# Exponentials on VectorE as a sum of two terms, masks over pairs of steps, 109 steps instead of 99

## The chip, the cores and the metric

The kernel runs on one core of a Trainium2 chip. The core has engines that run side by side: TensorE (PE, with its weight loads as PEld), VectorE (DVE), ScalarE (ACT), GpSimd (POOL) and SyncE (SP, which here only starts transfers). Each works through its own queue in order and waits on semaphores of the others. The metric is the time of one execution on the device in microseconds (us); lower is better. A profile is one traced execution.

## The reference, cut to what matters

Two attention layers read the same x (2048 rows, 512 columns, 32 heads of 16) and are mixed by a gate. A is linear attention with softmax features, B is full softmax attention.

```python
qkv = (x @ wqkv).reshape(B, S, 3, H, Dh)            # in both layers, each with its weights
# A: phi(q), phi(k) = softmax features of q @ w_phi, k @ w_phi (both signs, 32 per head)
num = phi_q @ (phi_k^T @ v);  den = phi_q . sum(phi_k) + 1e-6;  a = (num / den) @ wo_A
# B:
scores = einsum("bhqd,bhkd->bhqk", q, k) * (Dh ** -0.5)
b = einsum("bhqk,bhkd->bhqd", softmax(scores), v) @ wo_B
out = g * a + (1 - g) * b                           # g = sigmoid((x * gate_w).sum(-1))
```

B needs 32 x 2048 x 2048 exponentials. They are most of the work.

## The kernel before

**Tiling of B.** The work is cut into 32 sets: four chunks of 512 queries (`qc`), four groups of eight heads (`g`), and the even or odd heads of a group (`par`). A set has four heads and 16 steps, one for each 128 keys (`kt`). A step has two halves. In each half, TensorE writes the scores of two heads into a score buffer of PSUM (`R_r`, 128 x 1024 floats, three buffers; L736; `qk`). Then one of two engines takes the exponentials:

- ScalarE reads a score buffer and writes 128 x 1024 exponentials in bf16 to an `E` buffer (L755; ring `E_r`, six buffers; in the first set also memory that is not in use yet, `phiK` and `vA`).
- VectorE, for `NDVE` of the 16 steps of a set, builds the exponentials out of the bits of a bf16 number. L745 adds a constant to the scores, which were scaled so that the integer result, read as bf16, has the right exponent (`I`, two halves of a step in one buffer of 2048 columns). L760 keeps the exponent bits (`G`), L763 the mantissa bits (`F`), L766 squares `F`, L769 multiplies `I` by `F`. The exponential is the sum of three terms, I, G and F, of which the last two are weighted by `CPOLY`.

The sum itself is made by TensorE: the value products (`pv`; L791 for ScalarE's steps, L778 for VectorE's) multiply the exponentials by V with columns of ones beside it and accumulate all steps of a set in one PSUM bank (`O_r`, one buffer). VectorE's steps take three products of four matmuls each: I with `vB`, G and F with `vC`, a copy of V times `CPOLY` for the first four key steps (L518). At the end of a set VectorE copies the bank out (`OT`, L453), and it is transposed (L816) and divided by its sum (L820, L827).

**Beside it** run the projections (L459), the features of A (exponentials on ScalarE L621, their sums on VectorE L623 and L627, their division on GpSimd L628), checks of the denominators on GpSimd (L625, L822 to L826) and the output (L867 to L885). A query tile has one copy of q per head of four with the other rows zero: GpSimd clears three of the four query buffers (L430), transfers scatter q into them (L503, `qsp`); the first query tile is instead built by VectorE by four products with masks (L494).

**What sets the order.** The queues are written out by a scheduler in Python (`_Sched`): every operation has an engine, an assumed duration, a due time (`prio`), a time before which it is not placed (`nb`) and the buffers it takes. The scheduler plays these through with its own clock and puts each operation on its engine's queue. Only the resulting order and the waits for semaphores reach the chip, not the planned times. `next_pe` picks TensorE's next operation by a rank: scores for ScalarE when fewer than two or three lie ahead of it, then scores for VectorE, then the rest by due time. `T0`, `tset` and `ut` give the calendar of the sets; `LEAD` is how much earlier than its place in the set a VectorE step begins.

```python
NDVE = [0, 1] + [3, 3, 3, 4] * 7 + [3, 4]
R_r = _Slots([ps[:, 1024 * i:1024 * (i + 1)] for i in range(3)])
O_r = _Slots([ps[:, 3072:3584]])
```

At the end a check of the denominators (`flag`) decides whether a slow second version runs; it did not in the profile.

Of the kernel before, what the change touches and what calls it, by code (L numbers as in the profile page):

```python
# [6 lines left out]
BF16 = mybir.dt.bfloat16  # L7
# [6 lines left out]
D = 512  # L14
H = 32
# [11 lines left out]
CPOLY = 0.65625  # L27
KAP = 2.1484825
# [4 lines left out]
ND = 4  # L33
# [3 lines left out]
NDVE = [0, 1] + [3, 3, 3, 4] * 7 + [3, 4]  # L37
LEAD = 5.0
EXTRA = 1.2
SLACK = 0.8  # L40
# [14 lines left out]
T0 = 12.0  # L55

# [20 lines left out]
class _Op:  # L77
    __slots__ = ("eng", "fn", "dur", "prio", "deps", "tiles", "mode", "name", "dma",
                 "n_open", "users", "after", "late", "start", "end", "count", "sem", "vc", "seq", "est", "parts", "feeds")


class _Sched:
# [5 lines left out]
    def __init__(self):  # L88
        self.ops = []

    def add(self, eng, prio, dur, fn, deps=(), tiles=(), mode=None, name="", dma=None, nb=0.0, after=(), parts=1, feeds=None):
# [5 lines left out]
        o.mode, o.name, o.dma, o.est = mode, name, dma, nb  # L97
        o.late = 0.0 if name.startswith("qk") else SLACK
        o.users, o.start, o.end, o.count, o.sem, o.vc = [], None, None, None, None, None
        o.seq, o.parts, o.feeds = len(self.ops), parts, feeds  # L100
        for t in o.tiles:
            t.ops.append(o)
        self.ops.append(o)
        return o

    def next_pe(self, cands, first, last_mode):


        def pending(eng, at):
            return sum(1 for x in self.fed[eng] if x is None or x > at)  # L110

        def rank(w, o):
            if o.feeds == "act" and pending("act", w) < (3 if last_mode == "row" else 2):
                return 0
            if o.feeds == "dve" and pending("dve", w) < 1:
                return 1
            return 2
        now = [(w, o) for w, o in cands if w <= first + 0.02]
        soon = [w for w, o in cands if o.feeds == "act" and first + 0.02 < w and pending("act", w) < 2]
        if soon:  # L120
            limit = min(soon) + HOLD
            fit = [(w, o) for w, o in now if o.feeds or w + o.dur <= limit]
# [4 lines left out]
        return min(now, key=lambda c: (rank(*c), c[1].prio + (STAY if c[1].mode != last_mode else 0.0), c[1].seq))  # L127

# [184 lines left out]
def _build(ctx, nc, A_x, A_wqkv, A_w_phi, A_wo, B_wqkv, B_wo, gate_w, out):  # L313
# [20 lines left out]
    vC_ = sb([128, ND, VROW], name="vC")  # L334
    vB, vC = (v[:, :, 0:H * VW].rearrange("p t (h c) -> p t h c", c=VW) for v in (vB_, vC_))
# [70 lines left out]
    def pool(prio, dur, fn, deps=(), name=""):  # L406
        return add("pool", prio, dur, fn, deps=deps, name=name)
# [15 lines left out]
    op_vcones = pool(-99, 0.3, lambda e: e.memset(vC[:, :, :, 16:18], CPOLY), name="vcones")  # L423
    op_vpad = [pool(-99, 0.2, lambda e, v=v: e.memset(v[:, :, H * VW:VROW], 0.0), name="vpad") for v in (vB_, vC_)]
# [4 lines left out]
    op_vAones = pool(-96, 0.3, lambda e: e.memset(vA[:].rearrange("p t g c -> p (t g) c")[:, :, 64:65], 1.0))  # L429
    op_qz = [pool(-96 - 0.1 * i, 2.0, lambda e, i=i: e.memset(q_r.aps[i][:], 0.0), name="qz") for i in range(1, 4)]  # L430
    m1 = pool(-95, 0.3, lambda e: e.iota(t2.rearrange("p (g c) -> p g c", c=16), [[-32, 4], [0, 16]],
                                         channel_multiplier=1, allow_small_or_imprecise_dtypes=True))
# [37 lines left out]
    ev_v, ev_vc = {}, {}  # L470
# [36 lines left out]
    def v_proj(st, n, prio):  # L507

        tile = _Tile(M_r if n == 1 else R_r)
        fs = [fill(prio, tile, 512 * i, lambda t, i=i: xT[:, t, 128 * (st + i):128 * (st + i + 1)], lambda t: W_Bv[:, t, :],  # L510
                   op_x[st // 4] + [op_wv], f"vf{st}") for i in range(n)]
        use_wv.extend(fs)
        src = lambda: tile.ap[:, 0:512 * n].rearrange("p (t h d) -> p t h d", t=n, d=16)
        e1 = evac("dve", prio, lambda: vB[:, st:st + n, :, 0:16], src, fs, [tile], n=512 * n, name=f"vev{st}")
        for i in range(n):
            ev_v[st + i] = e1
        if st < ND:
            e2 = add("dve", prio + 0.1, 0.14 + 0.54 * n, lambda e: e.tensor_single_scalar(  # L518
                vC[:, st:st + n, :, 0:16], src(), CPOLY, ALU.mult), deps=fs, tiles=[tile], name=f"vcev{st}")
            for i in range(n):  # L520
                ev_vc[st + i] = e2
# [190 lines left out]
    for qc in range(QC):  # L712
        for g in range(KT):
            ob = _Tile(oB_r)
            norm = []
            for par in range(2):
# [5 lines left out]
                steps = [(ta + (k - nd) * (tb - ta) / (NT - nd), k, False) for k in range(nd, NT)]  # L722
                steps += [(ta + (k + 0.5) * (tb - ta) / nd - LEAD, k, True) for k in range(nd)]
                due = []
                for at, kt, vec in sorted(steps):
                    exps, es = [], []
                    if vec:
                        I, F, G = _Tile(I_r), _Tile(F_r), _Tile(G_r)
                    for pair in range(2):
# [11 lines left out]
                        when = at + pair * (1.3 if vec else 0.95)  # L741
                        q = add("pe", when - (0.0 if vec else RUSH), 0.22, qk, deps=[ev_k[g, kt // 4]] + (ev_q[g, qc][pair * 2:pair * 2 + 2] if len(ev_q[g, qc]) > 1 else ev_q[g, qc]), tiles=[r, qt], mode="row",
                                name=f"qk{nset}.{kt}", feeds="dve" if vec else "act", after=last_di if vec else last_qk, nb=at - 2.0 if vec else 0.0)
                        if vec:
                            last_di = [add("dve", when - 6, 1.19, lambda e, r=r, I=I, pair=pair: e.tensor_scalar(  # L745
                                I.ap[:, 1024 * pair:1024 * (pair + 1)], r.ap, EXP_B, 0.0, op0=ALU.add, op1=ALU.max),
# [11 lines left out]
                    if vec:  # L758
                        pd = at - 1
                        d2 = add("dve", pd - 0.1, 0.7, lambda e, I=I, G=G: e.tensor_scalar(  # L760
                            G.ap, I.ap, -128, 0x0040, op0=ALU.bitwise_and, op1=ALU.bitwise_or),
                            deps=exps, tiles=[I, G], name="de")
                        d1 = add("dve", pd, 0.7, lambda e, I=I, F=F: e.tensor_scalar(  # L763
                            F.ap, I.ap, 0x007F, 0x3F00, op0=ALU.bitwise_and, op1=ALU.bitwise_or),
                            deps=exps, tiles=[I, F], name="dm")
                        d3 = add("dve", pd, 1.22, lambda e, F=F: e.tensor_tensor(  # L766
                            F.ap.bitcast(BF16), F.ap.bitcast(BF16), F.ap.bitcast(BF16), ALU.mult),
                            deps=[d1], tiles=[F], name="dq")
                        d4 = add("dve", pd, 1.22, lambda e, I=I, F=F: e.tensor_tensor(  # L769
                            F.ap.bitcast(BF16), I.ap.bitcast(BF16), F.ap.bitcast(BF16), ALU.mult),  # L770
                            deps=[d3], tiles=[I, F], name="dw")

                        def pv(e, k, kt=kt, g=g, par=par, O=O, w=(I, G, F), first=False, last=False):
                            ins = None
                            val = vB_ if k == 0 else vC_
                            for s in range(4):
                                h = 8 * g + 2 * s + par
                                ins = e.matmul(O.ap[32 * s:32 * s + 32, :], lhsT=val[:, kt, VW * h:VW * h + 32],  # L778
                                               rhs=w[k].ap.bitcast(BF16)[:, 1024 * (s % 2) + 512 * (s // 2):][:, 0:512],
                                               start=first, stop=last, tile_position=(0, 32 * s),  # L780
                                               skip_group_check=True)
                            return ins
# [3 lines left out]
                    else:  # L786
                        def pv(e, es=es, kt=kt, g=g, par=par, O=O, first=False, last=False):
# [288 lines left out]
```

## Time and profile before

| | |
|---|---|
| median of 3 runs | 854.78 us (853.93 to 854.96) |
| profiled execution, its own time | 855.09 us |
| span of its trace | 853.2 us |
| ScalarE's exponentials in B (L755) | 802 into E buffers, 16 into `phiK`, 8 into `vA` |
| VectorE's steps | 99 (198 conversions, 99 of each of four others) |
| ScalarE, first 20 us / last 13.2 us | 5.85 / 4.01 us busy |
| value matmuls into `O_r` | 1652 for ScalarE's steps, 1188 for VectorE's |

The page gives each engine's busy time, then the costliest groups of instructions: line, engine, operation, output and input tile with shape, count, busy time in us and mean of one in ns, then the idle time of that engine just before them and what ended it. Busy times and means count an instruction from its start to its end; neighbours on one engine overlap a little, so the mean of one can be more than the distance from one to the next. The list of waits names who waited for whom, with the total in us, how many times, and the longest. Times in the timeline are from the start of the span.

### The profile page before, as it was taken

What the parts mean: (1) busy time and instruction counts of PE and PEld (TensorE: products, weight loads), DVE (VectorE), ACT (ScalarE), POOL (GpSimd) and SP (SyncE); (2) the same over time, 40 slices, a digit from 0 to 9 for tenths busy, and PEclk for the clock granted to TensorE, in tenths of its full rate; (3) what the DMA queues carried; (4) which work ended last, traced back from release to release, by engine and by line L of the source; (5) the groups of instructions that cost most, each with busy time, mean ns of one, the idle gap of its engine ahead of it and who ended that gap; (6) DMA issues with size and microseconds to landing.
All of it is one profiled execution on the core that took longest, in us unless ns stands there. A gap on an engine that the chain in (4) does not pass through costs nothing.

```text
span 853.2 us, 14410 instructions
## 1 busy us (share of the span) xinstructions
PE 750.0 (88%) x5971; PEld 233.0 (27%) x6040; DVE 773.9 (91%) x894; ACT 801.0 (94%) x901; POOL 170.1 (20%) x197
## 2 busy tenths in 40 slices
PE   7999999988989888889888999889998999888786
PEld 2233322222222222223222222222222222222222
DVE  4256999999999999999999999999999999999994
ACT  3969999999999889999999999999999999999895
POOL 7010011223322331012022202411122201310010
PEclk8999999999999999999999999999999999999999
DMA  9000000000000000000311101110112101110000
GB/s 223 25 7 2 8 6 1 8 7 7 7 1 13 1 13 1 7 14 7 76 26 38 26 13 38 25 39 19 25 20 45 26 17 27 27 39 1 7 1 29
DMA packets 55928, 19.64 MB, mean 23 GB/s; under 512 B 48304, under 2 KB 55856, under 8 KB 55856
## 3 DMA queue, kind: packets, MB, share of 16 engines
q1 hardware_dynamic: 52960, 17.06, 9.3%
q10 hardware_dynamic: 2640, 1.57, 0.7%
q8 instruction: 49, 0.80, 0.4%
q14 instruction: 23, 0.19, 0.1%
q0 software_dynamic: 256, 0.02, 0.0%
HBM read 3.69 MB, written 2.10 MB: 7 GB/s over the span
## 4 chain that ended last, share of the span: by engine, by line
ACT 57%; DVE 26%; PE 15%; issue 2%; DVEq 0%
ACT E L755 54%; DVE D L745 6%; PE ps L736 5%; DVE D L766 4%; DVE D L769 3%; DVE D L763 3%; DVE ss L623 3%; PE ps L459 3%; PE ps L791 2%; PE ps L867 2%; DVE D L760 2%; ACT WAT L621 2%; PE ps L778 1%; ACT phiK L755 1%; DVE ss L627 1%
## 5 line engine op out<-in xcount | busy, mean ns | idle before, releaser
L755 ACT ACTIVATE E<-ps 128x1024 bf16<-128x1024 f32 x802 | 747.6, 1141 | 27.0 <-PE ps L791 18.4
L736 PE MATMUL ps<-q,kT 64*128 64x512 bf16 x2048 | 374.1, 387 | 77.3 <-ACT E L755 51.3
L745 DVE TENSOR_SCALAR D<-ps 128x1024 int16<-128x1024 f32 x198 | 240.3, 1214 | 18.5 <-PE ps L736 17.9
L736 PEld LDWEIGHTS ps<-q,kT 64*128 64x128 bf16 x2048 | 91.0, 93 | 316.1 <-ACT E L755 229.4
L791 PE MATMUL ps<-E,vB 128*32 128x512 bf16 x1604 | 156.6, 389 | 5.8 <-issue 3.0
L766 DVE TENSOR_TENSOR D<-D 128x2048 bf16<-128x2048 bf16 x99 | 129.8, 1311 | 0.3
L769 DVE TENSOR_TENSOR D<-D 128x2048 bf16<-128x2048 bf16 x99 | 124.7, 1260 | 0.2
L822 POOL TENSOR_TENSOR acc<-acc,rB 128x16 f32<-128x16 f32 x32 | 25.9, 810 | 302.4 <-DVE rB L820 302.4
L625 POOL TENSOR_TENSOR acc<-acc,ss 128x64 f32<-128x64 f32 x32 | 26.8, 837 | 288.4 <-DVE ss L623 288.4
L778 PE MATMUL ps<-D,vC 128*32 128x512 bf16 x792 | 79.1, 390 | 3.1 <-issue 2.3
L763 DVE TENSOR_SCALAR D<-D 128x2048 int16<-128x2048 int16 x99 | 78.0, 788 | 0.0
L760 DVE TENSOR_SCALAR D<-D 128x2048 int16<-128x2048 int16 x99 | 74.8, 756 | 1.4
L791 PEld LDWEIGHTS ps<-E,vB 128*32 128x32 bf16 x1604 | 40.0, 93 | 86.0 <-issue 77.0
L459 PE MATMUL ps<-xT,WB 128*128 128x512 bf16 x110 | 42.6, 401 | 2.7 <-issue 0.8
L628 POOL TENSOR_TENSOR WB<-WAT,ss 128x1024 bf16<-128x1024 bf16 x16 | 38.8, 2427 | 6.5 <-DVE ss L627 6.5
L778 PE MATMUL ps<-D,vB 128*32 128x512 bf16 x396 | 39.7, 391 | 0.4 <-issue 0.3
L623 DVE TENSOR_REDUCE ss<-WAT 128x64 f32<-128x1024 bf16 x32 | 38.7, 1210 | 1.2 <-ACT WAT L621 1.2
L621 ACT ACTIVATE WAT<-ps 128x512 bf16<-128x512 f32 x64 | 37.9, 701 | 1.9 <-PE ps L459 1.0
L459 PE MATMUL ps<-Wp,xT 128*128 128x512 bf16 x99 | 38.2, 389 | 0.9 <-DVE oB L827 0.5
L628 POOL TENSOR_TENSOR phiK<-WAT,ss 128x1024 bf16<-128x1024 bf16 x16 | 34.2, 2138 | 11.6 <-DVE ss L627 11.6
L816 PE MATMUL ps<-ident,OT 128*128 128x128 f32 x128 | 32.3, 309 | 0.8 <-DVE vA L453 0.3
L453 DVE CAST vB<-ps 128x1024 bf16<-128x1024 f32 x8 | 9.8, 1225 | 22.8 <-PE ps L459 22.8
(104 smaller groups left out, 439.3 us busy)
## 6 DMA issues: line engine op xcount, KB each, us to landing
out_dram<-Wp SPq DMA_DIRECT2D x16, 128.0 KB, 1.7
q<-qs SPq DMA_DIRECT2D x120, 16.0 KB, 1.8
WB<-in_B_wqkv_dram ACTq DMA_DIRECT2D x2, 384.0 KB, 10.6
D<-in_A_x_dram SPq DMA_DIRECT2D x1, 512.0 KB, 4.7
WB<-in_B_wqkv_dram ACTq DMA_DIRECT2D x1, 512.0 KB, 9.5
WAv<-in_A_wqkv_dram SPq DMA_DIRECT2D x1, 512.0 KB, 4.1
phiK<-in_A_wo_dram SPq DMA_DIRECT2D x1, 512.0 KB, 3.7
phiK<-in_B_wo_dram SPq DMA_DIRECT2D x1, 512.0 KB, 4.7
```

The lines of the kernel that those rows point to most:

```text
L459: f = add("pe", prio - rush + 0.01 * t, MM, lambda e, t=t: e.matmul(tile.ap[:, off:off + 512], lhsT=lhs(t), rhs=rhs(t), start=(t == 0), st ...
L623: o6 = add("dve", prio + 5, 1.2, lambda e: e.tensor_reduce(ss.ap[:, 0, :], ee.ap.rearrange("p (g f) -> p g f", f=DH), AX.X, ALU.add), deps ...
L628: return add("pool", prio + 7, 2.0, lambda e: e.tensor_tensor(dst().rearrange("p (g f) -> p g f", f=DH), ee.ap.rearrange("p (g f) -> p g f ...
L736: ins = e.matmul(r.ap[:, 512 * i:512 * (i + 1)], lhsT=kT[p0:p0 + 64, g, 128 * kt:128 * (kt + 1)], rhs=qt.ap[p0:p0 + 64, 2 * pair + par, :] ...
L745: last_di = [add("dve", when - 6, 1.19, lambda e, r=r, I=I, pair=pair: e.tensor_scalar(I.ap[:, 1024 * pair:1024 * (pair + 1)], r.ap, EXP_B ...
L755: exps.append(add("act", when, 0.935, lambda e, r=r, E=E: e.activation(E.ap, r.ap, ACTF.Exp, scale=EXP_SCALE), deps=[q], tiles=[r, E], nam ...
L760: d2 = add("dve", pd - 0.1, 0.7, lambda e, I=I, G=G: e.tensor_scalar(G.ap, I.ap, -128, 0x0040, op0=ALU.bitwise_and, op1=ALU.bitwise_or), d ...
L763: d1 = add("dve", pd, 0.7, lambda e, I=I, F=F: e.tensor_scalar(F.ap, I.ap, 0x007F, 0x3F00, op0=ALU.bitwise_and, op1=ALU.bitwise_or), deps= ...
L766: d3 = add("dve", pd, 1.22, lambda e, F=F: e.tensor_tensor(F.ap.bitcast(BF16), F.ap.bitcast(BF16), F.ap.bitcast(BF16), ALU.mult), deps=[d1 ...
L769: d4 = add("dve", pd, 1.22, lambda e, I=I, F=F: e.tensor_tensor(F.ap.bitcast(BF16), I.ap.bitcast(BF16), F.ap.bitcast(BF16), ALU.mult), dep ...
L778: ins = e.matmul(O.ap[32 * s:32 * s + 32, :], lhsT=val[:, kt, VW * h:VW * h + 32], rhs=w[k].ap.bitcast(BF16)[:, 1024 * (s % 2) + 512 * (s ...
L791: ins = e.matmul(O.ap[32 * s:32 * s + 32, :], lhsT=vB_[:, kt, VW * h:VW * h + 32], rhs=es[s % 2].ap[:, 512 * (s // 2):512 * (s // 2 + 1)], ...
```

## The change

- `NDVE` goes from 99 to 109 steps on VectorE: sets of 4, 3, 4, 4, 3 steps after the first two.
- The exponential becomes a sum of two terms: `F` (mantissa bits) times `I`, and the exponent bits of `I` with its lowest bit set, written over `I` itself. The square is dropped, and so are `G`, `CPOLY` and `vC`. Both terms are multiplied with `vB`, so a VectorE step has two value products.
- Up to two steps form a pack (`WIDE`): the two masks run over 4096 columns for a pair, 2048 for a step that is left over. Conversions and products stay per half and per step. `I` has two buffers of 4096 columns, `F` one.
- `E_r` has eight buffers instead of six. When at least `FULL` of them are held in the scheduler's clock (a number that is never reached with eight), an operation that frees an E buffer would be ranked earlier.
- `LEAD` is 6 instead of 5.
- In the scheduler's clock, GpSimd's clears of `Wbd` and of small tiles are not placed before 14 us and those of the query buffers not before 17 us.

```diff
-CPOLY = 0.65625
-KAP = 2.1484825
+KAP = 1.5071
-NDVE = [0, 1] + [3, 3, 3, 4] * 7 + [3, 4]
-LEAD = 5.0
+NDVE = [0, 1] + [4, 3, 4, 4, 3] * 6
+LEAD = 6.0
+WIDE = 2
+FULL = 9
+LATER = 14.0
...
+            if short and o.frees:
+                return 0.5
...
+        short = self.held(first) >= FULL
...
-    E_r = ring(6, [128, 1024], name="E")
-    D_all = [sb([128, 2048], I16, name="D")[:] for _ in range(6)]
-    I_r, F_r, G_r = (_Slots(D_all[2 * i:2 * i + 2]) for i in range(3))
+    E_r = ring(8, [128, 1024], name="E")
+    D_wide = [sb([128, 4096], I16, name="D")[:] for _ in range(3)]
+    D_all = [d[:, 2048 * i:2048 * (i + 1)] for d in D_wide for i in range(2)]
+    sch.stock = E_r
+    I_r, F_r = _Slots(D_wide[0:2]), _Slots(D_wide[2:3])
...
-    op_vcones = pool(-99, 0.3, lambda e: e.memset(vC[:, :, :, 16:18], CPOLY), name="vcones")
...
-    op_wbd0 = pool(-98, 0.6, lambda e: e.memset(Wbd[:], 0.0))
+    op_wbd0 = pool(-98, 0.6, lambda e: e.memset(Wbd[:], 0.0), nb=LATER)
...
-    op_qz = [pool(-96 - 0.1 * i, 2.0, lambda e, i=i: e.memset(q_r.aps[i][:], 0.0), name="qz") for i in range(1, 4)]
+    op_qz = [pool(-96 - 0.1 * i, 2.0, lambda e, i=i: e.memset(q_r.aps[i][:], 0.0), name="qz", nb=LATER + 3.0) for i in range(1, 4)]
...
-                steps += [(ta + (k + 0.5) * (tb - ta) / nd - LEAD, k, True) for k in range(nd)]
+                packs = [tuple(range(k, min(k + WIDE, nd))) for k in range(0, nd, WIDE)]
+                steps += [(ta + ((ks[0] + ks[-1] + 1) / 2) * (tb - ta) / nd - LEAD, ks, True) for ks in packs]
...
-                        d2 = add("dve", pd - 0.1, 0.7, lambda e, I=I, G=G: e.tensor_scalar(
-                            G.ap, I.ap, -128, 0x0040, op0=ALU.bitwise_and, op1=ALU.bitwise_or),
-                            deps=exps, tiles=[I, G], name="de")
-                        d1 = add("dve", pd, 0.7, lambda e, I=I, F=F: e.tensor_scalar(
-                            F.ap, I.ap, 0x007F, 0x3F00, op0=ALU.bitwise_and, op1=ALU.bitwise_or),
+                        n = 2048 * nk
+                        d1 = add("dve", pd, 0.15 + 0.55 * nk, lambda e, I=I, F=F, n=n: e.tensor_scalar(
+                            F.ap[:, 0:n], I.ap[:, 0:n], 0x007F, 0x3F00, op0=ALU.bitwise_and, op1=ALU.bitwise_or),
                             deps=exps, tiles=[I, F], name="dm")
-                        d3 = add("dve", pd, 1.22, lambda e, F=F: e.tensor_tensor(
-                            F.ap.bitcast(BF16), F.ap.bitcast(BF16), F.ap.bitcast(BF16), ALU.mult),
-                            deps=[d1], tiles=[F], name="dq")
-                        d4 = add("dve", pd, 1.22, lambda e, I=I, F=F: e.tensor_tensor(
-                            F.ap.bitcast(BF16), I.ap.bitcast(BF16), F.ap.bitcast(BF16), ALU.mult),
-                            deps=[d3], tiles=[I, F], name="dw")
+                        d4 = [add("dve", pd + 0.01 * y, 1.22, lambda e, I=I, F=F, lo=2048 * y: e.tensor_tensor(
+                            F.ap[:, lo:lo + 2048].bitcast(BF16), I.ap[:, lo:lo + 2048].bitcast(BF16),
+                            F.ap[:, lo:lo + 2048].bitcast(BF16), ALU.mult),
+                            deps=[d1], tiles=[I, F], name="dw") for y in range(nk)]
+                        d2 = add("dve", pd + 0.1, 0.15 + 0.55 * nk, lambda e, I=I, n=n: e.tensor_scalar(
+                            I.ap[:, 0:n], I.ap[:, 0:n], -128, 0x0001, op0=ALU.bitwise_and, op1=ALU.bitwise_or),
+                            deps=d4, tiles=[I], name="de")
...
-                        due.append((at + 4, lambda e, pv=pv, **kw: pv(e, 0, **kw), [ev_v[kt], op_vones] + exps, [I, O]))
-                        due.append((at + 4.5, lambda e, pv=pv, **kw: pv(e, 1, **kw), [d2, ev_vc[kt], op_vcones], [G, O]))
-                        due.append((at + LEAD + 2, lambda e, pv=pv, **kw: pv(e, 2, **kw), [d4, ev_vc[kt], op_vcones], [F, O]))
+                                due.append((at + LEAD + 2.5 * nk + x, pv, [done[kt - kts[0]], ev_v[kt], op_vones], [w, O]))
```

More of the change, by code (lines that the diff above doesn't have):

```diff
@@ L32 @@
 EXP_B = 128.0 * (127.0 - math.log2(KAP))
-ND = 4
 BIG = 1e30
@@ L78 @@
     __slots__ = ("eng", "fn", "dur", "prio", "deps", "tiles", "mode", "name", "dma",
-                 "n_open", "users", "after", "late", "start", "end", "count", "sem", "vc", "seq", "est", "parts", "feeds")
+                 "n_open", "users", "after", "late", "start", "end", "count", "sem", "vc", "seq", "est", "parts", "feeds", "frees")
 class _Sched:
@@ L89, in __init__ @@
         self.ops = []
+        self.stock = None
     def add(self, eng, prio, dur, fn, deps=(), tiles=(), mode=None, name="", dma=None, nb=0.0, after=(), parts=1, feeds=None):
@@ L97, in add @@
         o.mode, o.name, o.dma, o.est = mode, name, dma, nb
+        o.frees = any(t.slots is self.stock for t in tiles)
         o.late = 0.0 if name.startswith("qk") else SLACK
@@ L127, in next_pe, with held @@
         return min(now, key=lambda c: (rank(*c), c[1].prio + (STAY if c[1].mode != last_mode else 0.0), c[1].seq))
+    def held(self, at):
+        return sum(1 for t in self.stock.tenant if t is not None and (any(x.end is None for x in t.ops) or
+                                                                      max(x.end for x in t.ops) > at))
     def run(self):
@@ L333, in _build @@
     vB_ = sb([128, NT, VROW], name="vB")
-    vC_ = sb([128, ND, VROW], name="vC")
-    vB, vC = (v[:, :, 0:H * VW].rearrange("p t (h c) -> p t h c", c=VW) for v in (vB_, vC_))
+    vB = vB_[:, :, 0:H * VW].rearrange("p t (h c) -> p t h c", c=VW)
     vA = sb([128, NT, 8, 66], name="vA")
@@ L403, in _build, with pool @@
     op_gw = [dma("sp", -86 + 0.1 * t, 2.0, gw[:, t:t + 1], gwv[t], name="gw") for t in range(KT)]
-    def pool(prio, dur, fn, deps=(), name=""):
-        return add("pool", prio, dur, fn, deps=deps, name=name)
+    def pool(prio, dur, fn, deps=(), name="", nb=0.0):
+        return add("pool", prio, dur, fn, deps=deps, name=name, nb=nb)
     t0, t1, t2, t3 = (mtmp[:, i, :] for i in range(4))
@@ L422, in _build @@
     op_vones = pool(-99, 1.0, lambda e: e.memset(vB[:, :, :, 16:18], 1.0), name="vones")
-    op_vcones = pool(-99, 0.3, lambda e: e.memset(vC[:, :, :, 16:18], CPOLY), name="vcones")
-    op_vpad = [pool(-99, 0.2, lambda e, v=v: e.memset(v[:, :, H * VW:VROW], 0.0), name="vpad") for v in (vB_, vC_)]
-    op_wbd0 = pool(-98, 0.6, lambda e: e.memset(Wbd[:], 0.0))
+    op_vpad = [pool(-99, 0.2, lambda e: e.memset(vB_[:, :, H * VW:VROW], 0.0), name="vpad")]
+    op_wbd0 = pool(-98, 0.6, lambda e: e.memset(Wbd[:], 0.0), nb=LATER)
     wphi_v = A_w_phi.rearrange("(t j) i f -> j i t f", j=8)
@@ L428, in _build @@
               for j in range(8)]
-    op_vAones = pool(-96, 0.3, lambda e: e.memset(vA[:].rearrange("p t g c -> p (t g) c")[:, :, 64:65], 1.0))
-    op_qz = [pool(-96 - 0.1 * i, 2.0, lambda e, i=i: e.memset(q_r.aps[i][:], 0.0), name="qz") for i in range(1, 4)]
+    op_vAones = pool(-96, 0.3, lambda e: e.memset(vA[:].rearrange("p t g c -> p (t g) c")[:, :, 64:65], 1.0), nb=LATER)
+    op_qz = [pool(-96 - 0.1 * i, 2.0, lambda e, i=i: e.memset(q_r.aps[i][:], 0.0), name="qz", nb=LATER + 3.0) for i in range(1, 4)]
     m1 = pool(-95, 0.3, lambda e: e.iota(t2.rearrange("p (g c) -> p g c", c=16), [[-32, 4], [0, 16]],
-                                         channel_multiplier=1, allow_small_or_imprecise_dtypes=True))
+                                         channel_multiplier=1, allow_small_or_imprecise_dtypes=True), nb=LATER)
     m2 = pool(-94, 0.3, lambda e: e.tensor_single_scalar(t3, t2, 0.0, ALU.is_ge), [m1])
@@ L469, in _build @@
     use_wk, use_wv, use_wav, use_wp1 = [], [], [], []
-    ev_v, ev_vc = {}, {}
+    ev_v = {}
     def k_proj(g, c, prio, tile, off, eng="dve"):
@@ L516, in v_proj @@
             ev_v[st + i] = e1
[L517 to L521, printed above, removed]
     tw, tz = _Tile(M_r), _Tile(E_r)
@@ L606, in _build @@
     chk, chkB = [], []
-    op_one = pool(-94.3, 0.3, lambda e: e.memset(ones32[:], 1.0))
+    op_one = pool(-94.3, 0.3, lambda e: e.memset(ones32[:], 1.0), nb=LATER)
     accA, accB, okB, tmpB = acc[:, 0:64], acc[:, 64:80], acc[:, 96:112], acc[:, 112:128]
-    op_acc0 = pool(-94.5, 0.2, lambda e: e.memset(acc[:, 0:80], 0.0))
-    op_acc = pool(-94.4, 0.2, lambda e: e.memset(acc[:, 96:112], 1.0), [op_acc0])
+    op_acc0 = pool(-94.5, 0.2, lambda e: e.memset(acc[:, 0:80], 0.0), nb=LATER)
+    op_acc = pool(-94.4, 0.2, lambda e: e.memset(acc[:, 96:112], 1.0), [op_acc0], nb=LATER)
     def phi(prio, w, st, dst, dst_deps, dst_tiles):
@@ L721, in _build @@
                 nset += 1
-                steps = [(ta + (k - nd) * (tb - ta) / (NT - nd), k, False) for k in range(nd, NT)]
-                steps += [(ta + (k + 0.5) * (tb - ta) / nd - LEAD, k, True) for k in range(nd)]
+                steps = [(ta + (k - nd) * (tb - ta) / (NT - nd), (k,), False) for k in range(nd, NT)]
+                packs = [tuple(range(k, min(k + WIDE, nd))) for k in range(0, nd, WIDE)]
+                steps += [(ta + ((ks[0] + ks[-1] + 1) / 2) * (tb - ta) / nd - LEAD, ks, True) for ks in packs]
                 due = []
-                for at, kt, vec in sorted(steps):
+                for at, kts, vec in sorted(steps):
                     exps, es = [], []
+                    nk = len(kts)
                     if vec:
-                        I, F, G = _Tile(I_r), _Tile(F_r), _Tile(G_r)
-                    for pair in range(2):
+                        I, F = _Tile(I_r), _Tile(F_r)
+                    for kt, pair in ((kt, pair) for kt in kts for pair in range(2)):
+                        part = 2 * (kt - kts[0]) + pair
                         r = _Tile(R_r)
@@ L740, in qk @@
                             return ins
-                        when = at + pair * (1.3 if vec else 0.95)
+                        when = at + (part * 1.3 if vec else pair * 0.95)
                         q = add("pe", when - (0.0 if vec else RUSH), 0.22, qk, deps=[ev_k[g, kt // 4]] + (ev_q[g, qc][pair * 2:pair * 2 + 2] if len(ev_q[g, qc]) > 1 else ev_q[g, qc]), tiles=[r, qt], mode="row",
@@ L744, in _build @@
                         if vec:
-                            last_di = [add("dve", when - 6, 1.19, lambda e, r=r, I=I, pair=pair: e.tensor_scalar(
-                                I.ap[:, 1024 * pair:1024 * (pair + 1)], r.ap, EXP_B, 0.0, op0=ALU.add, op1=ALU.max),
+                            last_di = [add("dve", when - 6, 1.19, lambda e, r=r, I=I, part=part: e.tensor_scalar(
+                                I.ap[:, 1024 * part:1024 * (part + 1)], r.ap, EXP_B, 0.0, op0=ALU.add, op1=ALU.max),
                                 deps=[q], tiles=[r, I], name=f"di{nset}.{kt}")]
@@ L766, in _build @@
-                        d3 = add("dve", pd, 1.22, lambda e, F=F: e.tensor_tensor(
-                            F.ap.bitcast(BF16), F.ap.bitcast(BF16), F.ap.bitcast(BF16), ALU.mult),
-                            deps=[d1], tiles=[F], name="dq")
-                        d4 = add("dve", pd, 1.22, lambda e, I=I, F=F: e.tensor_tensor(
-                            F.ap.bitcast(BF16), I.ap.bitcast(BF16), F.ap.bitcast(BF16), ALU.mult),
-                            deps=[d3], tiles=[I, F], name="dw")
[L773 to L782, printed above, removed]
@@ new lines, in _build, with pv @@
+                        for x, (w, done) in enumerate(((F, d4), (I, [d2] * nk))):
+                            for kt in kts:
+                                def pv(e, w=w, kt=kt, g=g, par=par, O=O, base=2048 * (kt - kts[0]), first=False, last=False):
+                                    ins = None
+                                    for s in range(4):
+                                        h = 8 * g + 2 * s + par
+                                        ins = e.matmul(O.ap[32 * s:32 * s + 32, :], lhsT=vB_[:, kt, VW * h:VW * h + 32],
+                                                       rhs=w.ap.bitcast(BF16)[:, base + 1024 * (s % 2) + 512 * (s // 2):][:, 0:512],
+                                                       start=first, stop=last, tile_position=(0, 32 * s),
+                                                       skip_group_check=True)
+                                    return ins
+                                due.append((at + LEAD + 2.5 * nk + x, pv, [done[kt - kts[0]], ev_v[kt], op_vones], [w, O]))
@@ L786, in _build @@
                     else:
+                        kt = kts[0]
                         def pv(e, es=es, kt=kt, g=g, par=par, O=O, first=False, last=False):
```

## The prediction

> **What bounds the kernel now.** I read the totals first, then the stretches, then each engine's waits, then the groups for prices. The totals:
>
> ```profile
> span 853.2 us, 14410 instructions
> PE 750.0 (88%) x5971; PEld 233.0 (27%) x6040; DVE 773.9 (91%) x894; ACT 801.0 (94%) x901; POOL 170.1 (20%) x197
> ```
>
> Two engines are near the span. The windows, with the columns PE, PEld, DVE, ACT, POOL, say where:
>
> ```profile
> core 0: us, PE busy (x) PEld busy (x) DVE busy (x) ACT busy (x) POOL busy (x), PEclk, DMA share, GB/s
> 60.00:100.00 40.00, 37.23 (x336) 12.88 (x336) 29.60 (x39) 40.00 (x46) 4.27 (x7) 1.00 0.02 5
> 100.00:840.00 740.00, 651.99 (x5317) 200.77 (x5373) 715.97 (x823) 717.74 (x808) 149.14 (x151) 1.00 0.08 18
> ```
>
> From 100 to 840 us ACT and DVE are each 97% busy: ACT is the limit and DVE, just as full, makes it wait. The clock column is 1.00, so the clock plays no part. What ACT waited for:
>
> ```profile
> ACT E L755 <- PE ps L791: 18.4, 12, 6.6
> ACT E L755 <- PE ps L736: 8.0, 14, 1.1
> ```
>
> The first line (us, times, longest) is an exponential without a free E buffer: the value product that frees it is late. One of its waits, 6.6, is in the start (46.4 to 53.0 us), so 11 others cost 11.8. The second is scores that come late. Prices are in the groups (busy, mean of one):
>
> ```profile
> L755 ACT ACTIVATE E<-ps 128x1024 bf16<-128x1024 f32 x802 | 747.6, 1141 | 27.0 <-PE ps L791 18.4 <-PE ps L736 8.0
> L745 DVE TENSOR_SCALAR D<-ps 128x1024 int16<-128x1024 f32 x198 | 240.3, 1214 | 18.5 <-PE ps L736 17.9
> L791 PE MATMUL ps<-E,vB 128*32 128x512 bf16 x1604 | 156.6, 389 | 5.8 <-issue 3.0
> L766 DVE TENSOR_TENSOR D<-D 128x2048 bf16<-128x2048 bf16 x99 | 129.8, 1311 | 0.3
> L769 DVE TENSOR_TENSOR D<-D 128x2048 bf16<-128x2048 bf16 x99 | 124.7, 1260 | 0.2
> L763 DVE TENSOR_SCALAR D<-D 128x2048 int16<-128x2048 int16 x99 | 78.0, 788 | 0.0
> L760 DVE TENSOR_SCALAR D<-D 128x2048 int16<-128x2048 int16 x99 | 74.8, 756 | 1.4
> ```
>
> For ACT and PE I divide busy time by count, since neighbours overlap: 0.932 us per exponential, 0.098 per value matmul. In the timeline a DVE instruction starts about 0.08 before the end of the one ahead, so each costs its mean less 0.08.
>
> **ACT.** 109 steps on DVE instead of 99 take 10 x 2 exponentials from ACT: 20 x 0.932 = 18.6 us. ACT is full from 60 us on, so all of it is on the path. **-18.6**.
>
> **DVE.** Before, the 594 instructions of the five lines cost 647.6 - 594 x 0.08 = 600.1 us. After, there are 218 conversions (x 1.134 = 247.2), 109 products (x 1.18, from L769, in place as they stay: 128.6), and masks over 48 pairs and 13 single steps: 26 narrow ones (x 0.69 = 17.9) and 96 of 4096 columns, a width no row has. The median of the 2048-column mask is 0.687 and that of the 512-column query mask L494 is 0.370. A line through these gives 1.11, twice the first gives 1.37. I take 1.24, plus the 0.085 by which the narrow masks' mean exceeds their median, less 0.08: 1.245 x 96 = 119.5. The new sum is 513.2; with the two scaled copies of V gone (L518, 2.3), DVE's work falls from 773.9 to about 685. The bounds move this by 12 us either way; DVE stays 13% below ACT's 782, so the width's price is not on the path. That the second mask writes over its own input costs nothing: the last L494 does so too and shows no more than the others' 0.33 to 0.37 once GpSimd is quiet.
>
> [...]
>
> **Per set.** One of 32 sets with 3 DVE steps needs 26 x 0.932 on ACT and 4 with 24; the 64 feature exponentials (L621, 37.9 us) add 1.2 to each: 25.4 and 23.6. DVE's other work is (773.9 - 600.1)/32 = 5.4. Before, a step cost 6.06, so the cycle 3, 3, 3, 4 took 99.8 us on ACT and 100.4 on DVE. After, a pair costs 4 x 1.134 + 2 x 1.245 + 2 x 1.18 = 9.4, a single 4.8, and the cycle 4, 3, 4, 4, 3 takes 121.6 on ACT and 111.8 on DVE. DVE has 8% of room, but within a 4-step set it needs 24.2 against ACT's 23.6.
>
> **PE.** Two value products per DVE step instead of three: 2840 value matmuls become 2484; 356 x 0.098 = 34.8 us less. PE (88% busy) binds only in the start; nothing is credited.
>
> **Waits for E.** In the order of PE's instructions, the product that frees an E buffer stands behind the scores of the exponential that needs it 26 times before and 8 times after (eight buffers instead of six do that; the new rank asks for nine held and so never acts). Two of each are in the start. 24 places cost 11.8 us, 0.49 each; 6 cost 2.9. **-8.9**; bounds 0 (other places turn late) and -11.8.
>
> **Waits for scores.** A score buffer that ACT's scores take was last read by a DVE conversion 55 times before, 42 after, and DVE has more room: 8.0 x 42/55 = 6.1. **-1.9**. The masks and products between two pairs' conversions are now a block of 2 x 1.245 + 2 x 1.18 = 4.85 us, against 3.80 before, in which a score buffer can stay held; so the bounds are -8 and +8.
>
> **The start.** The first query mask waits for GpSimd's clears:
>
> ```profile
> 10.26 5.15 DVE L494 TENSOR_SCALAR q<-q,masks 128x512 bf16<-128x512 bf16 x4
> 10.74 3.56 POOL L430 MEMSET q<- 128x2048 bf16 x2
> ```
>
> One of those four took 4.195 us, the others 0.33 to 0.37, and the first scores wait for it. The change holds the clears back only in the scheduler's clock. On POOL's queue nothing in front of them waits for anything later than before: the eight w_phi loads (4.27 us to issue) now stand ahead of all three clears, two clears of vC (0.32 and 0.15) are gone, one iota moved ahead. The clears end some 0.2 earlier, near 14.1, and still cover 10.26: -0.2, where a gap for the masks would give up to -3.9. The loads are needed at 60 us and the query scatter at 51, which hides the rest. Further on, two more E buffers let ACT do two more exponentials (1.86) ahead of the 6.6 us stall, while PE has two more K-projection matmuls (0.215 each in the timeline) and two more pairs of score matmuls (4 x 374.1/2048), 1.16 in all, to do before it ends: -0.7. **-0.9** together.
>
> **GpSimd beside DVE.** The same instruction by its neighbour:
>
> ```profile
> 300.50 0.62 DVE L760 TENSOR_SCALAR D<-D 128x2048 int16<-128x2048 int16 x1
> 301.04 2.41 DVE L763 TENSOR_SCALAR D<-D 128x2048 int16<-128x2048 int16 x1
> 300.65 2.25 POOL L628 TENSOR_TENSOR phiK<-WAT,ss 128x1024 bf16<-128x1024 bf16 x1 [1.34 <-DVE ss L627]
> ```
>
> Means less medians over the four SBUF lines come to about 31 us in all for 32 such feature products. I keep them (they are inside the prices above); DVE's room hides them from ACT.
>
> [...]
>
> **Sum.** The profiled execution took 855.09 (span 853.2 and 1.9 around it). 855.1 - 18.6 - 8.9 - 1.9 - 0.9 = 824.8; the median of the runs lies 0.3 below the profiled one: **824.5 us**.
>
> **Rivals.**
> - Stalls stay (0.28): the coarser packs undo what the buffers give. Only ACT's work and the start count: 855.1 - 18.6 - 0.9 - 0.3 = 835.3, up to 843 with waits for scores doubled. For it: the last value product of a set comes from DVE in 17 of 31 sets, 11 before, and the 4-step sets are tight. Against: DVE's 8% over a cycle.
> - The single F buffer turns into a wait (0.10, slower). The first mask of a pack needs F read by PE, and PE, in order, stands still at a value product whose DVE input is late, with ACT's scores behind it. If each of 61 packs costs ACT one wait of the size seen for late scores (8.0/14 = 0.57), that is 35 us: 824.5 + 35 = 859.5. It decides from 30.3/61 = 0.50 per pack. Against: PE waited for the last product L769 only six times before, 2.1 us in all.
> - Nearly every middle stall goes (0.08): 855.1 - 18.6 - 11.8 - 8.0 - 0.9 - 0.3 = 815.5.
>
> **Numbers.** The forecast has 0.50; 0.02 falls to the same time and 0.02 to a gain smaller than the rivals'. The range runs from 813 to 842, the lower end 2.5 below the third rival for the width's price and a gap in the clears; it leaves out the slower rival and the rest, some 0.2. Under 0.2%, 1.7 us, this measurement can't tell from no change. Faster: 0.50 + 0.28 + 0.08 + 0.02 = 0.88.
>
> **What would show it.** Right: ACT 782 busy, its idle time down from 52 to about 40; its waits for value products near 9 us instead of 18.4, one of them 5 to 6; DVE near 685 of 823 (83%); wide masks of 1.1 to 1.4; one query mask still near 4 us. Wrong: first masks that wait for PE, PE that stands long on D, ACT idle for 52 us or more.

## The result, and the profile after

The changed kernel took 831.61 us (median of 4 runs, 830.08 to 833.28), beside 854.75 for the kernel before: a ratio of 0.973 (0.971 to 0.976). The forecast was 824.5, the range 813 to 842. So the sign and the range held, but the gain was 23.1 us instead of 30.3, and the measured time lies nearer to the first rival's 835.3 than to the forecast. The profiled execution took 833.28 us (span 831.5), 1.7 above the median.

The totals of the page after:

```profile
span 831.5 us, 13591 instructions
PE 745.2 (90%) x5684; PEld 228.4 (27%) x5684; DVE 688.2 (83%) x747; ACT 782.4 (94%) x881; POOL 149.3 (18%) x195
```

ACT's 782.4 and DVE's 688.2 are the forecast's 782 and 685. ACT's idle time is 831.5 - 782.4 = 49.1 us, where 40 was expected and 52.2 stood before. The windows show where (same columns as before):

```profile
60.00:100.00 40.00, 38.06 (x315) 12.69 (x311) 26.92 (x33) 38.96 (x44) 1.95 (x7) 0.96 0.02 5
100.00:820.00 720.00, 649.14 (x5045) 196.87 (x5045) 634.61 (x683) 699.65 (x789) 130.76 (x151) 0.98 0.09 19
```

In the middle ACT is still 97% busy, DVE now 88%. DVE has the room that the forecast gave it, and ACT idles as much as before. The granted clock is 0.98 instead of 1.00. ACT's waits, and two lines of PE's queue that have no counterpart before (us, times, longest):

```profile
ACT E L764 <- PE ps L745: 19.8, 26, 3.1
ACT E L764 <- PE ps L800: 6.7, 2, 6.5
PE ps L745 <- DMA q<-qs: 7.3, 4, 2.2
PEld ps L745 <- DMA q<-qs: 1.7, 1, 1.7
```

The waits for value products (L800) fell from 18.4 to 6.7: what is left is the one in the start (6.5) and one of 0.2. The waits for scores (L745) rose from 8.0 to 19.8. The two cancel: 26.4 us before, 26.5 after. The last two lines are PE itself waiting for the query transfers `qsp`: four stands, 7.3 us in all. The PEld line is the weight load of one of these four (at 178.6 us) and does not add to them. The prices, from the groups:

```profile
L764 ACT ACTIVATE E<-ps 128x1024 bf16<-128x1024 f32 x782 | 728.9, 1144 | 27.1 <-PE ps L745 19.8
L754 DVE TENSOR_SCALAR D<-ps 128x1024 int16<-128x1024 f32 x218 | 264.9, 1215 | 64.3 <-PE ps L745 63.6
L770 DVE TENSOR_SCALAR D<-D 128x4096 int16<-128x4096 int16 x48 | 60.9, 1268 | 1.1 <-PE ps L787 0.3
L777 DVE TENSOR_SCALAR D<-D 128x4096 int16<-128x4096 int16 x48 | 63.5, 1324 | 0.0
```

Both wide masks are inside the 1.1 to 1.4 that was expected. What holds up the scores is seen in the timeline. SP issues the eight transfers of one query tile; PE then waits for the last of them (start, length, engine, line, operation, count, idle time ahead and its releaser):

```profile
408.06 5.97 SPq L514 DMA_DIRECT2D q<-qs  x8
415.42 0.39 PE L745 MATMUL ps<-q,kT 64*128 64x512 bf16 x2 [2.07 <-DMA q<-qs]
416.61 2.12 ACT L764 ACTIVATE E<-ps 128x1024 bf16<-128x1024 f32 x2 [1.64 <-PE ps L745]
419.22 5.61 ACT L764 ACTIVATE E<-ps 128x1024 bf16<-128x1024 f32 x6 [0.49 <-PE ps L745]
```

VectorE's copy of the projection ended at 408.03, and the scores could start 7.4 us later: 5.97 to issue eight transfers and about 1.4 more for the last to land. PE stood for 2.07 us and ACT lost 1.64, then 0.49 more. Five such places (at 179, 417, 522, 623 and 722 us) cost ACT 3.10, 1.64, 0.96, 1.18 and 2.10, 8.98 us in all. At the third of them the profile puts PE's stand of 1.26 us down to a reciprocal of VectorE that ended together with the transfers. The kernel before has no line of PE waiting for `q<-qs`. The reason is in the order: in PE's order fewer score pairs now stand between a projection and its first use, for the 15 tiles 9 to 65 before, 3 to 43 after. The five waits are at the five tiles with the fewest: 3, 8, 8, 9 and 10. Why the scheduler puts the projections closer is not shown. Their due times are counted in the calendar of the sets, by the same line in both kernels, and the sets got shorter by 20 of 826 exponentials only, 2.4%.

### The profile page after: what moved, and what is told of

Its sections match the earlier page's. It is cut to its first block, busy times and chain, and to the rows that moved or that the text cites. A ratio compares the mean times of both kernels' runs of the same rounds, so it can differ in the third digit from the quotient of the medians.

```text
span 831.5 us, 13591 instructions
## 1 busy us (share of the span) xinstructions
PE 745.2 (90%) x5684; PEld 228.4 (27%) x5684; DVE 688.2 (83%) x747; ACT 782.4 (94%) x881; POOL 149.3 (18%) x195
## 4 chain that ended last, share of the span: by engine, by line
ACT 59%; PE 20%; DVE 17%; SPq 2%; issue 1%; DMA 1%; DVEq 0%
ACT E L764 54%; PE ps L745 8%; DVE D L754 4%; PE ps L470 4%; DVE D L773 4%; PE ps L800 3%; SPq L514 2%; DVE D L770 2%; ACT WAT L627 2%; PE ps L787 2%; ACT phiK L764 2%; PE ps L876 2%; DVE ss L629 2%; DVE D L777 1%; ACT vA L764 1%
## 5 line engine op out<-in xcount | busy, mean ns | idle before, releaser
L764 ACT ACTIVATE E<-ps 128x1024 bf16<-128x1024 f32 x782 | 728.9, 1144 | 27.1 <-PE ps L745 19.8
L745 PE MATMUL ps<-q,kT 64*128 64x512 bf16 x2048 | 372.8, 390 | 69.9 <-ACT E L764 43.0
L754 DVE TENSOR_SCALAR D<-ps 128x1024 int16<-128x1024 f32 x218 | 264.9, 1215 | 64.3 <-PE ps L745 63.6
L745 PEld LDWEIGHTS ps<-q,kT 64*128 64x128 bf16 x2048 | 92.0, 93 | 306.0 <-ACT E L764 217.7
L800 PE MATMUL ps<-E,vB 128*32 128x512 bf16 x1564 | 154.7, 396 | 2.3 <-ACT E L764 0.8
L773 DVE TENSOR_TENSOR D<-D 128x2048 bf16<-128x2048 bf16 x109 | 138.8, 1292 | 0.5
L787 PE MATMUL ps<-D,vB 128*32 128x512 bf16 x872 | 83.3, 398 | 0.6 <-DVE D L773 0.6
L770 DVE TENSOR_SCALAR D<-D 128x4096 int16<-128x4096 int16 (+1 forms) x61 | 70.3, 1153 | 7.1 <-PE ps L787 6.0
L777 DVE TENSOR_SCALAR D<-D 128x4096 int16<-128x4096 int16 (+1 forms) x61 | 73.5, 1205 | 0.2
L631 POOL TENSOR_TENSOR acc<-acc,ss 128x64 f32<-128x64 f32 x32 | 21.0, 656 | 286.3 <-DVE ss L629 286.3
L831 POOL TENSOR_TENSOR acc<-acc,rB 128x16 f32<-128x16 f32 x32 | 18.0, 563 | 289.5 <-DVE rB L829 289.5
L800 PEld LDWEIGHTS ps<-E,vB 128*32 128x32 bf16 x1564 | 38.6, 93 | 92.6 <-issue 79.9
L470 PE MATMUL ps<-Wp,xT 128*128 128x512 bf16 x128 | 49.7, 394 | 0.1
L787 PEld LDWEIGHTS ps<-D,vB 128*32 128x32 bf16 x872 | 21.2, 95 | 38.0 <-issue 32.6
L876 PE MATMUL ps<-phiK 128*128 128x512 bf16 x88 | 30.4, 386 | 0.2 <-ACT E L764 0.2
```

Of the source, the lines that this page charges most:

```text
L470: f = add("pe", prio - rush + 0.01 * t, MM, lambda e, t=t: e.matmul(tile.ap[:, off:off + 512], lhsT=lhs(t), rhs=rhs(t), start=(t == 0), st ...
L745: ins = e.matmul(r.ap[:, 512 * i:512 * (i + 1)], lhsT=kT[p0:p0 + 64, g, 128 * kt:128 * (kt + 1)], rhs=qt.ap[p0:p0 + 64, 2 * pair + par, :] ...
L764: exps.append(add("act", when, 0.935, lambda e, r=r, E=E: e.activation(E.ap, r.ap, ACTF.Exp, scale=EXP_SCALE), deps=[q], tiles=[r, E], nam ...
L770: d1 = add("dve", pd, 0.15 + 0.55 * nk, lambda e, I=I, F=F, n=n: e.tensor_scalar(F.ap[:, 0:n], I.ap[:, 0:n], 0x007F, 0x3F00, op0=ALU.bitwi ...
L773: d4 = [add("dve", pd + 0.01 * y, 1.22, lambda e, I=I, F=F, lo=2048 * y: e.tensor_tensor(F.ap[:, lo:lo + 2048].bitcast(BF16), I.ap[:, lo:l ...
L777: d2 = add("dve", pd + 0.1, 0.15 + 0.55 * nk, lambda e, I=I, n=n: e.tensor_scalar(I.ap[:, 0:n], I.ap[:, 0:n], -128, 0x0001, op0=ALU.bitwis ...
```

## The experiments

Theory 1: the late query transfers are what the forecast missed. Theory 2: VectorE's longer instructions beside GpSimd, which the forecast called hidden, reach ACT. Rivals: the width of the packs makes the waits; the start holds the rest; the list of 109 steps is not worth its 18.6 us. Each run has five times, with the kernel before run beside it. The first four rows are from one chip and the last four from another; the kernel before took 853.97 and 854.04 us there. In the code of the halves, lines after L514 stand one lower, in that of the clears two.

| run | median, us (range) | ratio to before |
|---|---|---|
| changed kernel again | 829.94 (829.28 to 833.02) | 0.973 (0.972 to 0.975) |
| scatter in two halves | 821.64 (818.22 to 824.02) | 0.961 (0.959 to 0.962) |
| clears behind the masks | 827.98 (825.46 to 830.58) | 0.969 (0.967 to 0.971) |
| six E buffers | 825.12 (824.22 to 827.41) | 0.967 (0.965 to 0.968) |
| halves, six E buffers | 825.36 (822.77 to 825.75) | 0.966 (0.965 to 0.967) |
| halves, 99 steps | 839.05 (837.51 to 839.99) | 0.982 (0.980 to 0.983) |
| halves, narrow masks | 820.94 (818.84 to 822.39) | 0.961 (0.959 to 0.963) |
| halves, short feature products | 812.95 (810.26 to 814.91) | 0.952 (0.950 to 0.954) |

**The changed kernel again**, to have it beside the others.

> The changed kernel itself, as the measure for the others on this chip: 831.6 us within 2 of it, with some 9 us of ScalarE's idle time in five waits behind TensorE waiting for the query scatter (q<-qs).

829.94, with 15.8 us of waits for scores: these waits differ by 4 us between the two profiles of this kernel.

**The scatter in two halves.** A set uses the even or the odd heads of a group. The eight transfers become two operations of four, so that scores of even heads wait for four only. The order on PE, ACT, VectorE and GpSimd is the same instruction for instruction.

```diff
-                    for j in range(4) for a in range(2)]
-        ev_q[g, c] = [add("sp", prio, 2.0, split, deps=[ev] + op_qz, tiles=[qs, qt], name=f"qsp{g}{c}", dma=3.0, parts=8)]
+                    for j in js for a in range(2)]
+        ev_q[g, c] = [add("sp", prio + 0.001 * h, 2.0 - 2.0 * h, lambda e, h=h: split(e, (h, h + 2)), deps=[ev] + op_qz, tiles=[qs, qt],
+                          name=f"qsp{g}{c}", dma=3.0, parts=4) for h in range(2)]
...
```

The heads are j = 0 and 2 in the first operation, 1 and 3 in the second; scores of an even set depend on the first alone (`ev_q[g, qc][0:1 + par]`).

> The query scatter is handed out as two halves of four transfers, those for the even heads first, so that a group's first set waits for four transfers instead of eight (4 x 0.59 = 2.36 us earlier); the order on TensorE, ScalarE, VectorE and GpSimd is the changed kernel's, instruction for instruction. Theory 1 (late query scatter, and the lower clock after TensorE has stood, cost what the forecast missed): TensorE waited 9.0 us in five waits for q<-qs, the longest 2.2, so they go almost wholly; ScalarE gets back the 9.0 us of its five waits there and most of the 3.2 us of short waits right after: 820 to 824 us, the granted clock above 0.985. Theory 2 (the longer blocks of masks and products on VectorE cause the late scores; the wait for q only stands where another would): 830 to 833 us, the waits move to VectorE's conversions.

821.64: 8.3 us less by the medians. PE's waits for `q<-qs` are gone, and ACT's for scores are down to 10.7:

```profile
ACT E L765 <- PE ps L746: 10.7, 17, 1.7
PE ps L746 <- DVE D L755: 9.1, 18, 1.3
```

Since the order did not move, this shows theory 1. Not all of the 8.98 us came from the transfers: at the first place (179 us) ACT still waits 1.68 of the 3.10. The granted clock of these runs is a little higher, too: 0.988 to 0.998 beside 0.982 to 0.990. At 0.988 and 0.989 a run with halves took 824.02 us and one without 829.28, so some 5 us of the 8.3 are gained at the same clock. What is left of PE's waits is for conversions of VectorE (second line).

**Clears behind the masks.** The clears get the four query masks as dependencies, so that they are later on the chip, too.

```diff
+            for o in op_qz:
+                o.deps.extend(ms)
```

> GpSimd's three query clears wait for the four query masks of VectorE, so that they really come later; the order on the engines is unchanged. Both theories: the longest query mask falls from 3.9 us to about 0.35 and the first exponential starts at 11.5 to 12 us instead of 15.3. Theory A (the start is bound by TensorE's projections, which end ScalarE's wait at 53 us): the wait of 6.5 us grows by most of what the start gains, and the time falls by 0.5 to 1 us. Theory B (ScalarE's start is on the path): it falls by 3.5 us.

827.98, 2.0 less, with ranges that overlap, between the 0.5 to 1 of theory A and the 3.5 of theory B. The masks no longer stretch and ACT's first exponential comes 2.2 us earlier, yet the stall in the start ends where it did (the timeline of this run, DVE and then ACT):

```profile
10.90 1.27 DVE L505 TENSOR_SCALAR q<-q,masks 128x512 bf16<-128x512 bf16 x4
13.13 1.02 ACT L766 ACTIVATE phiK<-ps 128x1024 bf16<-128x1024 f32 x1 [2.58 <-PE ps L747]
53.02 3.77 ACT L766 ACTIVATE E<-ps 128x1024 bf16<-128x1024 f32 x4 [6.48 <-PE ps L802]
```

In the changed kernel the same three are 4.85 us of masks, 15.34 and 53.08. The wait at 53 did not grow, as theory A had it: it is 6.48 us in both profiles. ACT had lost its gain before that. Its run of ten exponentials began at 22.31 us here and at 22.61 there, after two more waits for PE, 1.31 and 0.39, while PE's granted clock in the first 20 us was 0.93 here and 1.00 there. So this run does not tell what the clears are worth at an even clock.

**Six E buffers**, on the changed kernel.

```diff
-    E_r = ring(8, [128, 1024], name="E")
+    E_r = ring(6, [128, 1024], name="E")
```

> The changed kernel with six E buffers instead of eight. In TensorE's order the product that frees a buffer then stands behind the scores that need it 16 times instead of 8. Theory 1 (the two buffers removed the waits for E): ScalarE waits 5 to 8 us more for value products, 836 to 840 us. Theory 2 (VectorE's room removed them, not the buffers): within 1.5 us of the changed kernel.

825.12: faster than with eight, a miss of all that was expected. The scheduler's order moved with the ring. With six buffers four of the five late query tiles were projected earlier (by the trace some 31, 14, 14 and 14 score pairs before their first use, where there had been 10, 9, 8 and 8), although no due time had changed. PE's waits for the transfers fell from 4.9 to 2.7 us, ACT's for scores from 15.8 to 8.2, while those for value products rose from 6.7 to 11.4. So this run mixes two effects. The next has the halves on both sides.

**Six E buffers with the halves.**

> Six E buffers and the query scatter in two halves, beside eight buffers with the same scatter (821.6 us). Theory 1 (the buffers are worth what the waits for value products show, and the earlier run with six was faster only because its order put the query projections earlier): 4 to 6 us slower, 825 to 828, with 11 us of waits for value products. Theory 2 (VectorE's room had made the buffers needless): 820 to 823.

825.36 against 821.64: with the halves the kernel with two more buffers is 3.7 us faster by the medians. The waits for value products agree, 11.4 with six and 6.7 with eight, but those for scores go the other way, 5.9 and 10.7:

```profile
ACT E L765 <- PE ps L801: 11.4, 5, 6.8
ACT E L765 <- PE ps L746: 5.9, 13, 0.9
```

The sums are 17.3 and 17.4, so the profiles don't show where the 3.7 us lie, and the orders differ. With six buffers the halves themselves brought nothing (825.12 without, 825.36 with).

**99 steps with the halves**: the old list `NDVE`, all else as in the halves.

> 99 VectorE steps, in the old list of sets, with everything else of the change and the scatter in two halves. Theory 1 (ScalarE is the limit): 20 exponentials of 0.932 us come back, 18.6 us, less 2 to 4 for waits that go with a lighter VectorE: 836 to 840 us. Theory 2 (VectorE and its blocks set the time): VectorE loses some 45 us of work, and the time stays at 819 to 824.

839.05, 17.4 more. ACT's busy time is 799.7 instead of 781.0 and its waits change by 2 us only:

```profile
ACT E L765 <- PE ps L746: 8.9, 16, 1.1
ACT E L765 <- PE ps L801: 6.5, 1, 6.5
```

So 17.4 of the 18.6 us of the list are on the path. The rest of the change, with the halves, is worth 854.0 - 839.05 = 15 us without it.

**Narrow masks with the halves**: `WIDE = 1`.

> Masks step by step (WIDE = 1) at 109 steps, scatter in two halves. VectorE gets 192 masks of 2048 columns for 96 of 4096, 192 x 0.69 - 96 x 1.23 = 14 us more work, up to some 702 us busy, below ScalarE's 782. Theory 1 (ScalarE is the limit, the width's price is not on the path): 819 to 824 us. Theory 2 (VectorE's length counts where sets have four steps): 829 to 836.

820.94, the same within the spread, although VectorE is 10.8 us busier (698.9). ACT's waits changed places: 2.8 for scores, 10.6 for value products. This order differs from that of pairs, so the run says only that the width's price is not on the path.

**Short feature products with the halves.** GpSimd divides only 32 of 1024 columns of the features of A; the other columns are left out. All else is queued as before.

```diff
-            dst().rearrange("p (g f) -> p g f", f=DH), ee.ap.rearrange("p (g f) -> p g f", f=DH),
+            dst().rearrange("p (g f) -> p g f", f=DH)[:, 0:2, :], ee.ap.rearrange("p (g f) -> p g f", f=DH)[:, 0:2, :],
```

> The scatter in two halves, and GpSimd's 32 feature products over 32 columns instead of 1024 (the rest of the features is left out); the order is unchanged. VectorE's 25 us of longer instructions beside GpSimd go. Theory 1 (the forecast's: VectorE's room hides them from ScalarE): within 1.5 us of 821.6. Theory 2 (a late conversion makes TensorE stand, and its clock falls after that): 815 to 818 us, fewer waits for scores, the granted clock nearer 1.

812.95, 8.7 us less than the halves, below the 815 to 818 of theory 2. Almost no wait for scores is left, nor PE's for conversions:

```profile
ACT E L765 <- PE ps L801: 6.7, 2, 6.5
ACT E L765 <- PE ps L746: 1.7, 1, 1.7
PE ps L746 <- DVE D L755: 2.1, 7, 0.5
```

VectorE's instructions lost their long cases (fastest, median and slowest in ns):

```profile
L774 DVE TENSOR_TENSOR D<-D x109: 1154/1217/2950, 59.3 to 797.4; 128x2048 bf16<-128x2048 bf16 x109
L771 DVE TENSOR_SCALAR D<-D x61: 678/1218/2626, 58.6 to 796.6; 128x4096 int16<-128x4096 int16 x48, 128x2048 int16<-128x2048 int16 x13
```

are the two with full feature products, and with the short ones

```profile
L774 DVE TENSOR_TENSOR D<-D x109: 1160/1216/1261, 58.6 to 785.3; 128x2048 bf16<-128x2048 bf16 x109
L771 DVE TENSOR_SCALAR D<-D x61: 683/1217/1289, 57.9 to 784.6; 128x4096 int16<-128x4096 int16 x48, 128x2048 int16<-128x2048 int16 x13
```

VectorE is 17.2 us less busy (670.9 against 688.1), and half of that came off the end. In the profile of the halves, 10 of ACT's 17 waits for scores, 5.3 us, end 4.6 to 9.2 us after a feature product began, and all 10 are gone. This shows theory 2 as far as the late conversions go; that the clock falls after them is not shown. Its size is rather 5 to 7 us than 8.7: another 3.0 us of those waits have no feature product near (2.0 at 89 to 92 us, where the granted clock from 60 to 100 us was 0.91, and 1.0 at 807 to 809 us). The profile of the short products, with a clock of 1.00 from 60 to 100 us, happens not to have them, and where runs of both had the same granted clock, 0.991, they took 821.64 and 821.68 beside 814.91 and 814.69. The short products also free their inputs and outputs earlier, but in neither profile does PE, ACT or VectorE wait for a feature product.

The two kernels with halves are the best versions that leave nothing out: 821.64 with pairs and 820.94 with single steps, some 10 us under the changed kernel. Whether the 109 steps could be had with the old sum of three terms was not measured, nor were 111 steps or query projections with earlier due times; by 6.06 us a step VectorE would need 773.9 + 60.6 = 834.5 us, so it would be the limit, but that is argued only.

## Why the prediction was right, and which term was mis-sized

**ACT, -18.6: right.** 801.0 to 782.4 in the profile, and 17.4 us by the list alone.

**Waits for E, -8.9: right in kind, measured -11.7**, close to the bound. Outside the start six late places were priced at 2.9; a single wait of 0.2 us is seen. The buffers account for 4.7 of it by the run with six and the halves (11.4 against 6.7); the rest came with the other order.

**Waits for scores, -1.9: this step failed; measured +11.8**, beyond its own bound of +8. It scaled the 8.0 us by the number of score buffers last read by a conversion, 42/55, as though a score buffer were all that scores wait for. They also need the query tile. The prediction dealt with the query scatter of one tile alone ("the query scatter at 51, which hides the rest") and not with the other 14, whose projections came closer to their first use in the new order. That is 8.3 us by the halves. The wait in each place is short, but it stops PE and so the scores for both engines. The 26 waits can be told apart by what lies beside them: 8.98 us at the five late query tiles, 3.2 where PE's granted clock was 0.50 right after four of these, 2.1 where it was 0.50 elsewhere, and 5.6 behind feature products. "The clock plays no part" was read from the kernel before (1.00 from 100 to 840 us) and did not hold for the one after (0.98 from 100 to 820 us).

**"DVE's room hides them from ACT": wrong.** The 31 us of contention were kept inside the prices, and DVE did have 12% to spare. Yet room over a set is no cover for one instruction that takes 2.95 us instead of 1.2: the conversion behind it is late, it holds a score buffer, and PE stands in front of ACT's scores. In the changed kernel near 376 us (timeline):

```profile
376.27 2.78 POOL L634 TENSOR_TENSOR WB<-WAT,ss 128x1024 bf16<-128x1024 bf16 x1 [1.27 <-DVE ss L633]
377.30 3.96 DVE L773 TENSOR_TENSOR D<-D 128x2048 bf16<-128x2048 bf16 x2
382.46 1.03 PE L745 MATMUL ps<-q,kT 64*128 64x512 bf16 x4 [1.26 <-DVE D L754]
383.53 1.02 ACT L764 ACTIVATE E<-ps 128x1024 bf16<-128x1024 f32 x1 [0.95 <-PE ps L745]
```

Two products that take 2.4 us elsewhere take 3.96, and some 5 us later ACT waits 0.95. The last two lines stand in a stretch with a granted clock near half (0.53 from 382 to 384 us); in the second profile of the same kernel that wait is 0.52. It was no new loss, since the kernel before had the same 32 products. There 12 of ACT's 14 waits for scores, 7.2 of the 8.0 us, end 4.6 to 7.8 us after a feature product began. The longest but one stands behind the product at 300.65 that the prediction shows (kernel before):

```profile
305.73 8.36 ACT L755 ACTIVATE E<-ps 128x1024 bf16<-128x1024 f32 x9 [1.02 <-PE ps L736]
```

So the 8.0 us that were scaled were for the most part these, and 5.6 of them were left in the changed kernel. The first of the two products above began at 377.30, after GpSimd's at 376.27, and took 2.83 us, until 1.08 us past the end of GpSimd's at 379.05. By what means the one holds up the other is not shown.

**The start, -0.9: measured -1.8.** By 53 us ACT has done two exponentials more (1.86), and its stall ends at 53.08 instead of 53.00: PE's 1.16 us of extra work did not show. The first masks were as forecast: one of 3.94 us, since the clears are not later on the chip (9.01 to 14.3).

**DVE, 685, and the width: right.** 688.2, which is 12% below ACT (the forecast's own 685 is 12% below 782, too, not 13%), and narrow masks change nothing. PE's lighter load, 745.2 us busy instead of 750.0, was credited nothing, and no run takes it alone.

**The rivals.** "Stalls stay" gave 835.3, and ACT's waits in front of E did stay (27.0 and 27.1 us), but not by its mechanism: value products are not late any more, and packs of one step are no faster. The single F buffer costs 6.0 us of DVE's time in three waits, 5.0 of them in one at 495 us, where ACT does not wait; it decides nothing.

The gap of 7.1 us to the forecast is then: 13.7 more for scores, 2.8 less for E, 0.9 less in the start, 1.4 because the median lies 1.7 below the profiled run and not 0.3, and 1.5 less as what remains, in ACT's other small waits: 13.7 - 2.8 - 0.9 - 1.4 - 1.5 = 7.1. The range held because it reached up to 842, past the first rival, and because four smaller terms erred the other way, not because the late transfers had been foreseen.

## What to carry to other kernels

When a change moves the order of the main loop, list every input of the step that feeds the bound engine, and compare for each the distance in the queue between its producer and its first use, before and after: a transfer that had just been early enough becomes late without being touched (here PE stood 7.3 us in four places for transfers that it had not waited for before). An engine's spare share over a whole stage covers no single long instruction if a buffer that others need is held behind it (here 12% of spare, and products of up to 2.95 us instead of 1.2); price such instructions by the longest case and by who stands behind it, not by the mean. Splitting a group of small transfers by who needs them first was worth 8.3 us here, two more buffers 3.7.

## What the runs showed of the hardware

In the profile of the changed kernel the granted clock fell to 0.50 in six stretches of 3.41 us and in one of 6.83 (720.0 to 726.8 us), with PE 89 to 100% busy in them. Windows of 2 us around the wait at 416 us (columns as in the windows above):

```profile
414.00:416.00 2.00, 0.58 (x10) 0.39 (x10) 1.79 (x3) 0.98 (x2) 0.00 (x0) 1.00 0.38 81
416.00:418.00 2.00, 2.00 (x20) 0.47 (x17) 1.75 (x2) 1.31 (x2) 0.00 (x0) 0.56 0.01 1
418.00:420.00 2.00, 2.00 (x17) 0.33 (x9) 1.36 (x2) 1.51 (x2) 0.00 (x0) 0.59 0.33 66
420.00:422.00 2.00, 1.90 (x16) 0.77 (x14) 0.68 (x2) 2.00 (x4) 0.43 (x2) 1.00 0.00 0
```

Taken as one window, 416.3 to 419.6 us has a clock of 0.50. PE had stood for 2.07 us just before, and ACT's second wait, of 0.49 us at 419, lies in that stretch. The length of a stand does not decide it alone. After the stand of 1.36 us that ended at 178.6 us the clock stayed at 1.00 (176 to 182 us), and from 85.2 to 88.5 and from 457.3 to 460.5 us it was 0.50, too, with no stand of PE over 0.6 us in the 10 us before. What sets it off in this kernel is not shown.
